# A decode training step with two attention and two MLP layers: five query-weight chunks instead of four stay on chip between the two backward passes

## The chip, the cores and the metric

The kernel runs on one core of a Trainium2 chip. The metric is the device time of one execution in microseconds (us). A core has five engines with queues of their own: PE (matrix multiply, with its weight loads shown as PEld), DVE (vector), ACT (scalar), POOL and SP. SP does no arithmetic here; it issues most of the transfers between the large memory and the on-chip memory. Sixteen DMA engines carry every transfer, whichever engine issued it. The profile counts times from the start of the span.

## What is computed

One token passes through attention A, MLP B, attention A and MLP B again, with shared weights, and then the gradients of everything are taken. Cut to what matters:

```python
def A(x, k_cache, v_cache, wq, wo):          # D=1024, 32 heads of 128, 4 groups, window 4096
    q = x @ wq                               # wq: 1024 x 4096
    k, v = the last 4096 rows of each cache
    o = softmax(q k^T * 128**-0.5) v
    return o @ wo                            # wo: 4096 x 1024

def B(x, w1, b1, w2):                        # w1: 1024 x 3584, w2: 3584 x 1024
    h = x @ w1 + b1
    return (h * tanh(softplus(h))) @ w2

x = x + A(layernorm(x)); x = x + B(layernorm(x))
x = x + A(layernorm(x)); x = x + B(layernorm(x))
# outputs: x, and by the chain rule from grad_out the gradients of
# x, k_cache, v_cache, wq, wo, w1, b1, w2 (all bf16)
```

The cache gradients have the full length of 32768 rows. Outside the window of 4096 they are zero, and those zeros have to be written: 56 stores of 1 MB.

## The kernel before

**The weights come in chunks of 1 MB.** wq is cut into eight chunks of 128 rows (all 4096 columns), wo into eight of 512 rows, w2 into seven of 512 rows. A chunk of wq, wo or w2 lands in a slot of `ring_t`, eight slots of 8 KB in each of the 128 partitions. The class `Ring` (line 38) keeps a list of loads in a fixed order, each with a key such as `("q", 2, 3)`: chunk 3 of the third use of wq. `pump` (line 51) issues the next load on SP's queue when a slot is free in the program's order; the slot's last reader is waited for by SP itself. `release` (line 80) gives a slot back and pumps. `keep` (line 76) gives a chunk a new key and no slot back, so a chunk stays on chip. `lend` (line 86) adds slots: when w1 is no longer needed, three slots are cut from its memory. In the profile a load into `ring_t` is called `ring<-in_...`, a load into a lent slot `W<-in_...`.

**The order of the loads** is written out once (lines 270 to 290). Its end is what matters here: wq for the second attention's backward pass (`("q", 2, t)`, eight chunks), w2 for the first MLP's backward pass (`("2", 1, c)`, seven), wo for the first attention's backward pass (`("o", 3, c)`, eight), and the rest of wq for the first attention's backward pass (`("q", 3, t)`). The chunks of wq that `KEEP_Q2` (line 268) lists are not loaded this last time.

**The stages of the second half, in the order of the program.**

1. The second attention's backward pass, `attn_bwd(1, ...)` (line 960). Its last part is the wq loop of line 918, which multiplies each chunk with the query gradient. For this the chunk's 128 x 128 blocks have to be transposed: PE transposes eight blocks into PSUM (line 452), DVE or ACT copies them back over the chunk in its slot (`evac`, lines 305 and 308, whichever has less work by a running tally), and PE multiplies with them (line 471). That is called turning a chunk. A chunk has four groups of eight blocks. In chunks 0 and 1 all four are turned; in chunks 2 to 7 one group is left and goes as a row dot on DVE (line 429), and three are turned. `later` (line 436) holds a few products back, so that PE has transposes to do while a copy runs. After its products a chunk is released, or, if `KEEP_Q2` lists it, kept in its turned form; its key goes into `turned_q`.
2. The first MLP's backward pass, first loop (line 1105): for each of the seven chunks of w2, the forward product that is still owed (`mlp_out`, line 700: 32 weight loads and matmuls), then `flush`, which runs the products and releases that were held back, then the same chunk's gradient by two row dots and two turned groups. So a chunk's slot comes back only after the next chunk's `mlp_out`.
3. The first MLP's backward pass, second loop (`dn_b0`, line 840) with w1, which is on chip. During it SP issues small copies that gather rows for the outer products (lines 986, 786, 828).
4. `ring.lend(lent)` (line 1119): three more slots.
5. The first attention's backward pass, `attn_bwd(0, ...)`: the wo loop (line 865), two stages with the cached keys and values, and the wq loop again (line 918). A chunk whose key is in `turned_q` is only multiplied.
6. The outer products that make the weights' and caches' gradients (from line 1180), copied out of PSUM by DVE and ACT and stored by SP.

**The zeros** are issued on POOL's queue by `zeros(n, after)` (line 256), so many at each of several points of the program, each after a named value is ready: 3 while the second attention's wq loop begins, 1 at the end of it, 2 before `dn_b0`, and 19 later.

Of the kernel before, what the change touches and what calls it, by code (L numbers as in the profile page):

```python
# [93 lines left out]
def kernel(  # L94
# [135 lines left out]
    def want_q(k, ts=range(8)):  # L230
        for t in ts:
            ring.want(("q", k, t), wq_v[:, t, :], [P, J])

    def want_o(k, cs=range(8), homes=()):
        for c in cs:
            own = homes[c].rearrange("p (k d) -> p k d", k=4) if c < len(homes) else None
            ring.want(("o", k, c), wo_v[:, c], [P, 4, D], own, [("K", c)] if own is not None else [])
# [27 lines left out]


    KEEP_Q = (5, 6, 7)
    KEEP_Q2 = (4, 5, 6, 7)
    EARLY_2 = (0, 1)
    MID_2 = (2, 3)  # L270
    W1S = W1[:].rearrange("p t f -> p (t f)")
# [17 lines left out]
    want_o(3)  # L289
    want_q(3, [t for t in range(8) if t not in KEEP_Q2])  # L290
    ring.pump()
# [344 lines left out]
    def conv(n, eng=None):  # L636
        for _ in range(n):
            conv_ev(conv_pe(1), eng)
# [318 lines left out]
    def dq3():  # L957
        zeros(3, DQC[:, 0, 1:2])

    g2 = attn_bwd(1, sA1, g3, ("o", 1), ("q", 2), KEEP_Q2,  # L960
                  dict(do=lambda c: conv(1), dp=dp3, dq=dq3, dn=lambda t: None),
# [256 lines left out]
```

## Time and profile before

| | |
|---|---|
| three runs | 458.6, 459.16, 459.25 us (median 459.16) |
| the profiled execution | 458.38 us, of which the span is 456.6 us |
| PE, DVE, ACT, POOL busy | 322.4, 257.5, 204.6, 38.5 us |
| bytes moved | 183.56 MB: 83.94 read, 98.62 written |
| second attention's wq loop | from 223 to 243 us |
| first MLP's w2 loop | from 246 to 275 us |
| `dn_b0` | from 276 to 283 us |
| first attention's wo loop | from 286 to 305 us |
| first attention's wq loop | from 318 to 334 us |
| last arithmetic instruction ends | 422.5 us |

How to read the profile: the page divides the span into 40 slices of 11.4 us. A digit is the busy share of an engine in a slice in tenths, and 9 stands for 90% or more. DMA is the mean busy share of the sixteen DMA engines. The granted clock is the share of its full rate that PE was given. The chain of waits starts at the last instruction and goes back, at each step to what released the instruction, or to the one before it on its engine. A timeline line gives the start, the duration, the engine, the line of the program, the operation, what it writes and reads, and how often it stands there in a row; in brackets is the idle time of the engine before it and what ended it. A line of SPq is the issue of a transfer on SP's queue, not the transfer. A transfer's landing is told by sixteen completion marks, one from each DMA engine; its reader waits for the last of them.

### The profile page before, as it was taken

Reading aid. Unit: us, or ns where it says so; the run is one execution under the profiler, and the core shown is the slowest. Engines: PE = TensorE matmul, PEld = TensorE weight load, DVE = VectorE, ACT = ScalarE, POOL = GpSimd, SP = SyncE. Lnnn points to the kernel's source line nnn. Section 1 sums busy time; section 2 is a strip of 40 time slices with the busy share of each in tenths; the row PEclk is TensorE's granted clock in tenths of the full one; section 3 lists DMA queues with packets and bytes.
Section 4 is the critical chain, followed back from the end, with each engine's and each line's share of the span. In section 5 each row is a group of like instructions: output and inputs, shape, how many; then the busy total and the mean of one; then the engine's idle time right before and its main releaser. Section 6 shows DMA issues by size and latency. Waiting matters only on the chain.

```text
span 456.6 us, 13914 instructions
## 1 busy us (share of the span) xinstructions
PE 322.4 (71%) x6225; PEld 258.9 (57%) x6225; DVE 257.5 (56%) x506; ACT 204.6 (45%) x239; POOL 38.5 (8%) x84
## 2 busy tenths in 40 slices
PE   3836543456698898987798868988978988899000
PEld 3735433456597897987798768976922222345000
DVE  4504737278441265846286556763769999989000
ACT  2501001011054277752283542761669999998000
POOL 1000000002031222102100001022130000000000
PEclk9955555555555599978598555995955555555555
DMA  8999999989999999999999979999999999999995
GB/s 334 421 421 421 417 421 419 420 317 422 421 417 423 419 415 416 393 416 418 421 423 425 417 284 342 390 391 420 421 417 420 416 421 419 424 421 418 407 408 227
DMA packets 28377, 183.56 MB, mean 402 GB/s; under 512 B 3706, under 2 KB 3734, under 8 KB 9494
## 3 DMA queue, kind: packets, MB, share of 16 engines
q1 hardware_dynamic: 20162, 123.94, 66.6%
q0 software_dynamic: 8064, 58.72, 31.1%
q8 instruction: 48, 0.79, 0.6%
q14 instruction: 11, 0.09, 0.0%
q10 hardware_dynamic: 92, 0.02, 0.0%
HBM read 83.94 MB, written 98.62 MB: 400 GB/s over the span
## 4 chain that ended last, share of the span: by engine, by line
PE 37%; DMA 28%; DVE 11%; ACT 10%; issue 6%; SPq 0%; ACTq 0%; DVEq 0%
DMA ring<-in_B_w_dram 13%; PE BIG L452 9%; PE TP L471 5%; DMA ring<-in_A_wq_dram 5%; DMA W<-in_A_wo_dram 4%; DMA W<-in_B_w_dram 4%; ACT ring L308 4%; PE wide L1073 4%; PE wide L1022 3%; DVE junk L429 3%; DMA W<-in_A_k_cache_dram 2%; ACT W L308 2%; PE BIG L628 2%; PE MV L648 2%; ACT KT L308 2%
## 5 line engine op out<-in xcount | busy, mean ns | idle before, releaser
L308 ACT COPY ring<-BIG 128x1024 bf16<-128x1024 bf16 x51 | 50.4, 1015 | 45.5 <-PE BIG L452 20.1
L452 PE MATMUL BIG<-ident_bf,ring 128*128 128x128 bf16 x664 | 58.8, 247 | 0.5 <-ACT ring L308 0.3
L1022 PE MATMUL wide<-W 2*128 2x512 bf16 x228 | 52.1, 598 | 9.3 <-ACT W L308 1.9
L452 PEld LDWEIGHTS <-ring 128*128 128x128 bf16 x768 | 55.9, 113 | 1.1 <-issue 0.6
L429 DVE CUSTOM_DVE_ANT_0 junk<-ring,SC 128x1024 bf16<-128x1024 bf16 x32 | 38.9, 1215 | 9.8 <-DMA ring<-in_B_w_dram 9.4
L1022 PEld LDWEIGHTS <-W 2*128 2x128 bf16 x240 | 12.5, 102 | 44.0 <-issue 42.9
L305 DVE CAST ring<-wide 128x1024 bf16<-128x1024 f32 (+1 forms) x29 | 33.7, 1201 | 3.2 <-PE wide L1022 1.4
L471 PEld LDWEIGHTS <-ring 128*128 128x128 bf16 x864 | 30.0, 98 | 7.2 <-issue 3.4
L308 ACT CAST ring<-wide 128x1024 bf16<-128x1024 f32 (+1 forms) x35 | 32.9, 1018 | 1.3 <-PE wide L1073 0.5
L264 POOL DMA_DIRECT2D out_dram<-zt x56 | 29.7, 534 | 37.6 <-DMA out_dram<-zt 37.1
L305 DVE COPY ring<-BIG 128x1024 bf16<-128x1024 bf16 x32 | 21.8, 690 | 17.7 <-PE BIG L452 15.7
L429 DVE CUSTOM_DVE_ANT_0 junk<-ring,DSX 128x1024 bf16<-128x1024 bf16 x24 | 29.4, 1224 | 0.8
L648 PE MATMUL MV<-NB,W 128*128 128x1 bf16 x448 | 16.4, 172 | 14.8 <-DMA W<-in_B_w_dram 12.8
L308 ACT COPY KT<-BIG 128x1024 bf16<-128x1024 bf16 x14 | 13.8, 1008 | 26.7 <-PE BIG L628 25.2
L648 PEld LDWEIGHTS <-W 128*128 128x128 bf16 x448 | 15.8, 118 | 15.6 <-DMA W<-in_B_w_dram 13.4
L514 PE MATMUL MV<-NA,ring 128*128 128x1 bf16 x512 | 15.1, 165 | 12.6 <-DMA ring<-in_A_wq_dram 11.2
L308 ACT COPY W<-BIG 128x1024 bf16<-128x1024 bf16 x21 | 20.7, 1014 | 5.0 <-PE BIG L452 4.4
L452 PE MATMUL BIG<-ident_bf,W 128*128 128x128 bf16 x288 | 22.3, 221 | 0.3 <-issue 0.3
L514 PEld LDWEIGHTS <-ring 128*128 128x128 bf16 x512 | 14.6, 104 | 13.3 <-DMA ring<-in_A_wq_dram 11.9
L305 DVE CAST VS<-wide 128x1024 bf16<-128x1024 f32 (+1 forms) x17 | 19.7, 1188 | 3.6 <-PE wide L1022 3.0
L1073 PE MATMUL wide<-W 32*128 32x256 bf16 x128 | 20.9, 402 | 0.9 <-ACT ring L308 0.8
L308 ACT CAST KT<-wide 128x1024 bf16<-128x1024 f32 x20 | 20.4, 1032 | 1.8 <-PE wide L1022 0.9
(258 smaller groups left out, 538.5 us busy)
## 6 DMA issues: line engine op xcount, KB each, us to landing
out_dram<-zt POOLq DMA_DIRECT2D x56, 1024.0 KB, 20.3
ring<-in_A_wq_dram SPq DMA_DIRECT2D x24, 1024.0 KB
ring<-in_A_wo_dram SPq DMA_DIRECT2D x14, 1024.0 KB
ring<-in_B_w_dram SPq DMA_DIRECT2D x13, 1024.0 KB
W<-in_A_wo_dram SPq DMA_DIRECT2D x10, 1024.0 KB
W<-in_B_w_dram SPq DMA_DIRECT2D x8, 896.0 KB
out_dram<-ring SPq DMA_DIRECT2D x7, 1024.0 KB
out_dram<-ring SPq DMA_DIRECT2D x13, 512.0 KB
```

The costliest lines, as they stand in the source:

```text
L264: nc.gpsimd.dma_start(dst, zt[:])
L305: nc.vector.tensor_copy(dst, src)
L308: nc.scalar.copy(dst, src)
L429: nc.vector.tensor_tensor_reduce(out=out, in0=a, in1=vec, scale=1.0, scalar=acc if i else 0.0, op0=ALU.mult, op1=ALU.add, accum_out=acc)
L452: nc.tensor.transpose(b[:, i * P:(i + 1) * P], block(w, i) if block else w[:, i * P:(i + 1) * P], ident_bf[:])
L471: nc.tensor.matmul(out, lhsT=w[:, i * P:(i + 1) * P], rhs=rhs_of(i), start=fresh[0], stop=last and i == n - 1, skip_group_check=True)
L514: nc.tensor.matmul(q_ps[:, h:h + 1], lhsT=ch[:, h * P:(h + 1) * P], rhs=NA[:, t, l:l + 1], start=(k == 0 and h == 0), stop=(k == TD - 1), ...
L628: nc.tensor.transpose(b[:, i * P:(i + 1) * P], T[:, g, 8 * b8 + i, :], ident_bf[:])
L648: nc.tensor.matmul(h_ps[:, fb:fb + 1], lhsT=f_block(W1[:, t], fb), rhs=NB[:, t, l:l + 1], start=(t == 0 and fb == 0), stop=(t == TD - 1), ...
L1022: nc.tensor.matmul(b[:, 512 * i:512 * i + 512], lhsT=R[at:at + 2, lo:lo + P], rhs=R[at:at + 2, ro + 512 * i:ro + 512 * i + 512], start=Tru ...
L1073: nc.tensor.matmul(b[:, k * 256:(k + 1) * 256], lhsT=RT[32 * g:32 * g + 32, a, tp, :], rhs=YS[32 * g:32 * g + 32, :], start=True, stop=Tru ...
```

## The change

`KEEP_Q2` gets one more member, chunk 3:

```diff
     KEEP_Q = (5, 6, 7)
-    KEEP_Q2 = (4, 5, 6, 7)
+    KEEP_Q2 = (3, 4, 5, 6, 7)
     EARLY_2 = (0, 1)
```

The tuple is used in two places. In the list of loads, the last use of wq asks for chunks 0 to 2 and no longer for chunk 3:

```python
    want_q(3, [t for t in range(8) if t not in KEEP_Q2])
```

In the second attention's wq loop, chunk 3 is kept in its turned form, so its slot isn't given back there; the first attention's wq loop multiplies with it without turning it, and gives the slot back:

```python
            if t in wq_keep:
                ring.keep(key, ("q", 3, t))
                turned_q.add(("q", 3, t))
            else:
                later(lambda key=key: ring.release(key))
```

From the second attention's wq loop to the first's, five of the eight slots are taken, and three are left to the chunks of w2 and wo, until three more are lent. By the order of the instructions on each engine, PE has 24 transposes and 24 weight loads less, DVE one copy and ACT two copies less, all in the first attention's wq loop. SP issues the seven loads of w2 as before, then three loads of wo instead of four before the small copies of stage 3, and after the lend five loads of wo and three of wq instead of four and four. The instructions of POOL are the same in number and order.

## The prediction

> **What bounds the kernel now.** I read the page's slices first, then the stretches around its only hole, then the chain of waits, then the timeline of the load queue. The page shows transfers nearly everywhere:
>
> ```profile
> span 456.6 us, 13914 instructions
> ...
> DMA  8999999989999999999999979999999999999995
> GB/s 334 421 421 421 417 421 419 420 317 422 421 417 423 419 415 416 393 416 418 421 423 425 417 284 342 390 391 420 421 417 420 416 421 419 424 421 418 407 408 227
> ```
>
> Only slices 24 to 27 (262 to 308 us) fall clearly short in the second half. Stretches (columns: us; busy us of PE, PEld, DVE, ACT, POOL; granted clock; DMA share; GB/s):
>
> ```profile
> 256.00:260.00 4.00, 2.94 (x59) 2.67 (x56) 2.23 (x4) 2.61 (x3) 0.00 (x0) 0.50 1.01 422
> 260.00:264.00 4.00, 3.17 (x64) 2.91 (x64) 2.46 (x4) 1.05 (x3) 0.00 (x0) 0.50 0.98 395
> 264.00:268.00 4.00, 2.71 (x62) 2.71 (x63) 2.46 (x4) 1.28 (x3) 0.00 (x0) 0.50 0.91 340
> 268.00:272.00 4.00, 2.14 (x57) 1.87 (x55) 1.55 (x3) 1.62 (x2) 0.00 (x0) 0.50 0.65 254
> 272.00:276.00 4.00, 2.38 (x33) 1.96 (x31) 1.52 (x6) 1.93 (x2) 0.31 (x2) 0.50 0.78 279
> 276.00:280.00 4.00, 4.00 (x127) 3.85 (x126) 3.35 (x9) 0.25 (x1) 0.93 (x2) 0.50 0.86 231
> ...
> 316.00:336.00 20.00, 17.64 (x360) 15.47 (x361) 13.01 (x28) 9.36 (x13) 4.93 (x12) 0.76 1.01 420
> 336.00:424.00 88.00, 74.51 (x394) 26.55 (x393) 77.38 (x72) 81.00 (x92) 2.80 (x6) 0.50 1.01 419
> 424.00:448.00 24.00, 0.00 (x0) 0.00 (x0) 0.00 (x0) 0.00 (x0) 0.00 (x0) 0.50 1.02 407
> ```
>
> The reader sees two regimes. From 288 us to 448 the sixteen DMA engines are full, and from 424 on no engine computes: stores alone set the end. From 260 to 288 they are not full, and something else sets the time. The chain of waits names it (start, us, what):
>
> ```profile
> 235.15 20.49 DMA ring<-in_B_w_dram
> ...
> 257.28 12.99 DMA ring<-in_B_w_dram
> 270.33 1.01 PE MV L700 x32
> ```
>
> These are chunks of w2 for the first MLP's backward loop (line 1105). Call them c0 to c6. c3 is issued at 235.15 and starts its matmuls at 255.69; c6 is issued at 257.28 and starts at 270.33. The load queue around them:
>
> ```profile
> 235.15 0.33 SPq L71 DMA_DIRECT2D ring<-in_B_w_dram  x1
> 250.66 0.33 SPq L71 DMA_DIRECT2D ring<-in_B_w_dram  x1
> 253.97 0.33 SPq L71 DMA_DIRECT2D ring<-in_B_w_dram  x1
> 257.28 0.33 SPq L71 DMA_DIRECT2D ring<-in_B_w_dram  x1
> ```
>
> c0 to c3 take the slots of wq chunks 0 to 3 (229.57 to 235.15); c4, c5, c6 take those of c0, c1, c2. A slot comes back about 1.55 us after the next chunk's matmuls begin (255.69 to 257.28, 270.33 to 271.84 for the slot that a wo chunk takes), because line 1108 flushes only there. The zero stores from POOL compete: the one issued at 245.83 lands 25.1 us later.
>
> **The change, part by part.**
>
> *Removed: one wq load.* 1.05 MB, at 421 GB/s 2.5 us of all engines. It pays only where the engines are full for want of nothing else. The instruction order shows where it goes: before line 1119 lends three slots, SP issues three wo loads instead of four, and after it five wo and three wq loads, where it issued four and four. So the saturated stretch keeps its eight loads, and the missing megabyte comes out of the stretch that has holes already. I count 0; its bound is -2.5.
>
> *Removed: three turns of wq chunk 3 in the first attention's wq loop (line 918).* PE loses 24 transposes and their weight loads, DVE one copy, ACT two. By the rows of that loop:
>
> ```profile
> 324.17 0.61 PE L452 MATMUL BIG<-ident_bf,ring 128*128 128x128 bf16 x8
> 324.24 0.69 DVE L305 COPY ring<-BIG 128x1024 bf16<-128x1024 bf16 x1 [0.32 <-PE BIG L452]
> 324.81 1.93 ACT L308 COPY ring<-BIG 128x1024 bf16<-128x1024 bf16 x2 [0.28 <-PE BIG L452]
> ```
>
> PE loses 3 x 0.61 = 1.83, DVE 0.69, ACT 1.93 us. A turned chunk takes 2.14 us there (row dots at 324.84 and 326.99), a kept one 1.27 (the row dots from 329.13, 330.38, 331.65 on, DVE's own pace), so the loop ends 0.87 us sooner. What covers it is the store and zero traffic of 316 to 336 (share 1.01): worth 0; without that cover -0.9.
>
> *Moved: five of eight ring slots are taken from 235 us on, so three and not four rotate.* c3 must wait for c0's slot: issued at 250.66, 15.5 us later than before. c0, c1, c2 and the releases at 250.66 and 253.97 don't depend on it. How long does c3 then take? The trace shows a load into an empty queue under the same zero traffic: wq chunk 0, issued at 188.91, whose completion marks (one for each DMA engine) run from 197.8 to 200.4, thus 8.9 to 11.5 us. Lower bound: the wo chunk issued at 262.20, when most engines had no zeros left, first mark at 266.6, thus 4.4. The consumer waits for the last mark, and one engine is some 8 us behind the others with zeros (the last zero's marks: fifteen by 262.7, one at 270.9), so I take 11.5: c3 starts at 262.2, not 255.69.
>
> The Trainium skill ("DMA: Bandwidth & Descriptors", Queues, rings and completion order) says that each engine takes turns between the queues that have work, and its Specifications give about 0.6 us to the first byte for SP's path. By that, an estimate: c3 would land after 0.6 us and one shared 5 us turn, near 256.3, and almost nothing would be lost (rival A). The wq row, twice as slow, speaks against it; the even sharing itself the trace bears out (loads land every 5 us at 255.7, 260.7, 265.3, 270.3 beside zeros).
>
> What is late next: PE's own pace. One chunk costs it 1.01 (L700) + 0.56 (L471) + 1.87 (L452) = 3.45 us at the halved clock. c4, issued at 253.97, is right behind c3. c5 is issued 1.55 us after c3 starts, at 263.8, c6 at 267.2; the zeros, which are fixed in number, ran alone while loads were away and are then nearly gone, so 4.4 us each suffice (268.2, 271.6). Hence starts at 262.2, 265.65, 269.1 and 272.55: c6 is 2.2 us late. Bounds: 0.6 (c3 after 6.9 us: 1.9 to the first packet, as below, and one shared turn of 5; then the slowest engine merely does the same packets in another order, and c6 comes after the last zero at 270.9) and 4 (c5 and c6 each another 1 us late in landing).
>
> Behind SP's waits for these slots stand, in order, the wo loads, the row copies of lines 986, 786 and 828, and the lent slots' loads. All move by the same 2.2 us, and none has a taker earlier: the first wo chunk, issued after c5's start (270.7) and not at 262.2, is first turned at 282.77 + 2.2. After the lend every chunk is one place later in the queue. wo chunk 6 then takes the place of chunk 7 (marks to 299.2, first use 299.55), chunk 7 that of wq chunk 0 (marks to 301.7, first use 302.24). That fits by 0.3 to 0.5 us; I count 0.
>
> *What of the 2.2 reaches the end.* The first lent load is issued at 284.69 and its packets can begin 1.9 us later (4.4 less 2.5 of transfer), at 286.6; after the change at 288.8. But the slowest engine was before still busy with zeros until 287.7 (their last mark), so it loses only 288.8 - 287.7 = 1.1 us, and it ends the kernel (last marks 453.9 on the second slowest, 455.3 on the slowest). From there on bytes are equal. The others lose 2.2 and end at 456.1; the slowest at 456.4.
>
> Sum: 0 + 0 + 1.1. The profiled execution took 458.38 us with a span of 456.6, so 459.5; the median of the runs is 459.16, 0.78 above it: **460.3 us**.
>
> **The rivals.**
>
> *A: the late load is absorbed.* If c3 takes its turn within 6.9 us (257.5), c6 is 0.6 us late, and the slowest engine gains 1.1 less 0.6: 459.16 - 0.5 = 458.7, no change to tell. For it: strict alternation on the slowest engine, which is never idle from 235 to 288. Against: the wq row.
>
> *B: the bytes count (not slower).* If the end is set by all bytes together, the missing 1.05 MB is worth 2.5 us: 456.7. For it: share 0.9 or more in nearly all slices. Against: the hole of 260 to 288, whose stretches are already 6.7 us short of 421 GB/s in sum; a load less there widens the hole unless the loop itself gets quicker.
>
> *C: the wo loads arrive late as well.* The margins of 0.3 and 0.5 us after the lend fail, PE stalls in the loop of line 865, slots come back later and the engines run dry near 300 us, where they are at 324 GB/s already: 2 us more, 462.5. Against: loads of 5 chunks are outstanding by then.
>
> That the change does nothing is excluded: the order has one wq load and 24 transposes fewer.
>
> **How the numbers follow.** Forecast 0.42, A 0.34, B 0.16, C 0.08. A measurement of this kernel can tell about 0.2% (0.9 us) from no change. Of the forecast, 0.03 lies within that bound, of A 0.02 below it. Faster: 0.16 + 0.02 = 0.18. Within: 0.32 + 0.03 = 0.35. Slower: 0.39 + 0.08 = 0.47. The range takes A and the bounds of the delay (0.6 to 4 us, thus -0.5 to +2.9, and 0.8 more below for part of B): 457.9 to 462.1; the forecast's own is 459.4 to 461.3.
>
> **What would show it.** Right: c3 issued near 250.7 and its matmuls at 260 to 263; chunk starts after it 3.4 us apart, no longer waiting for loads but PE-paced; the lent loads 1 to 3 us later; DMA share in 268 to 284 lower than before; from 290 on the same 420 GB/s; the first attention's wq loop 0.9 us shorter without effect. Wrong: c3 landing before 257.5 (A), an end earlier by 2 us with the lent loads on time (B), or PE waiting for wo loads between 290 and 305 (C).

## The result, and the profile after

| | before | after |
|---|---|---|
| median of ten runs each, on one chip | 458.98 us (458.41 to 459.9) | 460.16 us (459.74 to 462.1) |
| ratio | 1 | 1.0034, 95% interval 1.0022 to 1.0046 |
| profiled execution: span | 456.6 us | 458.3 us |
| w2 chunk c3: issued, first matmul | 235.15, 255.69 | 250.86, 259.91 |
| last w2 chunk c6: first matmul | 270.33 | 271.73 |
| first lent load issued | 284.69 | 287.27 |
| end of the first attention's wo loop | 305.6 | 308.8 |
| first attention's wq loop (line 332 to line 402) | 317.58 to 334.24 | 321.78 to 337.05 |
| last completion mark of all | 455.3 | 457.0 |

The kernel became slower: by 0.34% in the ratio (1.6 us), by 1.2 us in the medians and by 1.7 us in the spans of the two profiles. Two cautions for reading what follows. The ratios of the record aren't the ratios of the medians. And only one execution of each kernel is profiled: those of e1, e5 and e8 are the fastest of their runs, 1.2 to 1.4 us below the median, and the w2 loop starts anywhere from 244.2 us (e1) to 252.7 us (e2), though the instructions ahead of it are the same in these two and in the kernel after (247.0). A difference of a few us between single rows of two profiles is therefore not by itself the edit's doing. The slices of the page after:

```profile
span 458.3 us, 13855 instructions
...
DMA  8999999989999999999999779999999999999996
GB/s 331 421 420 419 420 420 418 420 317 421 420 417 421 422 413 415 410 400 420 423 424 423 294 275 339 347 404 422 420 417 416 416 419 420 422 420 415 407 408 252
```

There is still one hole in the second half, but it begins a slice earlier. Slice 23 (252 to 263 us) moved 417 GB/s before and moves 294 now. The stretches of the profile after (us; busy us of PE, PEld, DVE, ACT, POOL; granted clock; DMA share; GB/s):

```profile
256.00:260.00 4.00, 0.10 (x4) 0.09 (x4) 0.00 (x1) 1.17 (x2) 0.00 (x0) 0.50 0.88 358
260.00:264.00 4.00, 3.08 (x64) 2.82 (x64) 2.46 (x4) 1.73 (x2) 0.00 (x0) 0.50 0.51 150
264.00:268.00 4.00, 3.03 (x64) 2.91 (x64) 2.46 (x4) 0.83 (x2) 0.00 (x0) 0.50 0.53 203
268.00:272.00 4.00, 3.37 (x75) 3.24 (x74) 2.85 (x5) 2.13 (x3) 0.00 (x0) 0.50 0.80 274
272.00:276.00 4.00, 3.46 (x69) 3.03 (x66) 2.06 (x4) 2.61 (x4) 0.00 (x0) 0.50 0.86 313
276.00:280.00 4.00, 2.77 (x84) 2.69 (x84) 2.29 (x9) 0.41 (x1) 1.25 (x3) 0.50 0.93 295
...
288.00:292.00 4.00, 4.00 (x53) 3.60 (x51) 2.17 (x4) 1.49 (x3) 0.00 (x0) 0.66 0.90 292
316.00:336.00 20.00, 16.91 (x437) 15.86 (x437) 12.34 (x22) 5.98 (x8) 3.70 (x10) 0.67 1.01 419
336.00:424.00 88.00, 76.89 (x404) 27.33 (x403) 77.77 (x79) 82.62 (x96) 4.02 (x9) 0.50 1.01 418
424.00:448.00 24.00, 0.23 (x2) 0.00 (x0) 1.49 (x2) 0.58 (x1) 0.00 (x0) 0.50 1.02 408
```

From 256 to 260 PE does almost nothing (0.10 us of 4; before 2.94): it waits for c3. From 260 to 268 PE works about as much as before, but the DMA engines stand half idle (0.51 and 0.53, before 0.98 and 0.91): with three slots there is nothing more that SP may issue, and the zeros are used up but for the last completion mark of the last piece (267.2). From 316 us on the two profiles are alike: full engines, then stores alone. The timeline of the w2 loop, with the first lines of line 700 for each chunk. Before, c3 to c6:

```profile
255.69 1.01 PE L700 MATMUL MV<-AC,ring 128*128 128x1 bf16 x32
260.69 1.02 PE L700 MATMUL MV<-AC,ring 128*128 128x1 bf16 x32 [1.75 <-DMA ring<-in_B_w_dram]
265.29 1.01 PE L700 MATMUL MV<-AC,ring 128*128 128x1 bf16 x32 [1.44 <-DMA ring<-in_B_w_dram]
270.33 1.01 PE L700 MATMUL MV<-AC,ring 128*128 128x1 bf16 x32 [1.86 <-DMA ring<-in_B_w_dram]
```

After, the issues of SP and c2 to c6:

```profile
250.86 15.96 SPq L71 DMA_DIRECT2D ring<-in_B_w_dram  x4
252.84 1.01 PE L700 MATMUL MV<-AC,ring 128*128 128x1 bf16 x32 [0.33 <-DMA ring<-in_B_w_dram]
259.91 1.01 PE L700 MATMUL MV<-AC,ring 128*128 128x1 bf16 x32 [3.90 <-DMA ring<-in_B_w_dram]
264.97 1.02 PE L700 MATMUL MV<-AC,ring 128*128 128x1 bf16 x32 [1.88 <-DMA ring<-in_B_w_dram]
268.77 1.01 PE L700 MATMUL MV<-AC,ring 128*128 128x1 bf16 x32 [0.63 <-DMA ring<-in_B_w_dram]
...
271.73 1.04 PE L700 MATMUL MV<-AC,ring 128*128 128x1 bf16 x32
```

c3 is issued at 250.86, when c0's slot comes back. Its sixteen completion marks run from 256.1 to 259.9, so it took 5.2 us on the quickest DMA engine and 9.0 on the slowest, and PE waited 3.9 us. The marks spread over the whole time between (the last two came at 259.5 and 259.9). Behind the loop SP issues the small copies and then the lent loads:

```profile
280.63 1.68 SPq L986 DMA_DIRECT2D W<-W  x2
282.42 0.84 SPq L786 DMA_DIRECT2D W<-dr_AC  x1
283.32 0.89 SPq L786 DMA_DIRECT2D W<-dr_NB  x1
284.26 0.71 SPq L786 DMA_DIRECT2D W<-dr_OC  x1
285.01 0.50 SPq L786 DMA_DIRECT2D W<-dr_NA  x1
285.61 1.54 SPq L828 DMA_DIRECT2D W<-W  x2
287.27 2.29 SPq L71 DMA_DIRECT2D W<-in_A_wo_dram  x3
```

The copies begin 1.74 us later than before (278.89 there) and the first lent load 2.58 later: SP spends 6.64 us on the copies and not 5.80.

**Two ways to add it up.** The first is the prediction's: the end of the span follows the issue of the first lent load, 171.9 us behind it before (456.6 - 284.69) and 171.0 after. The second is an own count over the packet records: the time in which all sixteen engines would have carried what they carried, and the rest, idle time. In the hole, from 236 to 308 us, the mean idle time grew from 3.7 to 7.7 us; one load of 2.5 us fell away; 4.0 - 2.5 = 1.5 us, against 1.7 in the span. (A plain sum of the packet times, which reaches a share of 1.02 where the engines are full, gives 2.9 and 6.9: the same growth.) In the other rows of the table below this second sum misses the span by up to 1.4 us, in e2 by 2.1 and in e3 by 4.4, so it tells where time is lost and proves no price. The argument rests on the first.

### The profile page after: what moved, and what is told of

The parts are those of the page before. It is cut to its first block, busy times and chain, and to the rows that moved or that the text cites. A ratio compares the mean times of both kernels' runs of the same rounds, so it can differ in the third digit from the quotient of the medians.

```text
span 458.3 us, 13855 instructions
## 1 busy us (share of the span) xinstructions
PE 316.8 (69%) x6201; PEld 253.1 (55%) x6201; DVE 256.9 (56%) x505; ACT 202.8 (44%) x237; POOL 38.5 (8%) x84
## 5 line engine op out<-in xcount | busy, mean ns | idle before, releaser
L308 ACT COPY ring<-BIG 128x1024 bf16<-128x1024 bf16 x49 | 48.4, 1014 | 46.7 <-PE BIG L452 22.5
L452 PE MATMUL BIG<-ident_bf,ring 128*128 128x128 bf16 x624 | 52.8, 240 | 1.5 <-issue 1.2
L452 PEld LDWEIGHTS <-ring 128*128 128x128 bf16 x712 | 49.6, 110 | 2.2 <-issue 1.7
L471 PEld LDWEIGHTS <-ring 128*128 128x128 bf16 x832 | 28.4, 98 | 8.9 <-issue 4.8
L305 DVE COPY ring<-BIG 128x1024 bf16<-128x1024 bf16 x29 | 19.8, 689 | 16.6 <-PE BIG L452 15.1
L648 PE MATMUL MV<-NB,W 128*128 128x1 bf16 x448 | 16.5, 172 | 15.1 <-DMA W<-in_B_w_dram 7.6
L514 PEld LDWEIGHTS <-ring 128*128 128x128 bf16 x512 | 14.8, 104 | 14.2 <-DMA ring<-in_A_wq_dram 11.2
```

The lines of the kernel that those rows point to most:

```text
L305: nc.vector.tensor_copy(dst, src)
L308: nc.scalar.copy(dst, src)
L452: nc.tensor.transpose(b[:, i * P:(i + 1) * P], block(w, i) if block else w[:, i * P:(i + 1) * P], ident_bf[:])
L471: nc.tensor.matmul(out, lhsT=w[:, i * P:(i + 1) * P], rhs=rhs_of(i), start=fresh[0], stop=last and i == n - 1, skip_group_check=True)
L514: nc.tensor.matmul(q_ps[:, h:h + 1], lhsT=ch[:, h * P:(h + 1) * P], rhs=NA[:, t, l:l + 1], start=(k == 0 and h == 0), stop=(k == TD - 1), ...
L648: nc.tensor.matmul(h_ps[:, fb:fb + 1], lhsT=f_block(W1[:, t], fb), rhs=NB[:, t, l:l + 1], start=(t == 0 and fb == 0), stop=(t == TD - 1), ...
```

## The experiments

Ratios are to the kernel before, with 95% intervals. "Idle" is the own count from 236 to 308 us in the profiled execution.

| run | ratio | first lent load | span | span less lent load | idle |
|---|---|---|---|---|---|
| before | 1 | 284.69 | 456.6 | 171.9 | 3.7 |
| after | 1.0034 (1.0022 to 1.0046) | 287.27 | 458.3 | 171.0 | 7.7 |
| e1_slot_withheld | 1.0087 (1.0068 to 1.0107) | 286.45 | 459.8 | 173.4 | 7.3 |
| e2_turn_again | 1.0039 (1.0023 to 1.0055) | 288.75 | 459.9 | 171.2 | 7.4 |
| k6_six_kept | 1.0337 (1.0305 to 1.0368) | 300.33 | 471.7 | 171.4 | 22.4 |
| k3_three_kept | 1.0059 (1.0046 to 1.0072) | 288.88 | 459.9 | 171.0 | 4.8 |
| e5_zeros_after_chunk_4 | 1.0023 (1.0004 to 1.0042) | 284.61 | 456.4 | 171.8 | 6.6 |
| e6, the same on before | 1.0021 (0.9999 to 1.0043) | 287.32 | 457.9 | 170.6 | 6.2 |
| e10_two_zeros_later | 1.0055 (1.0041 to 1.0069) | 288.51 | 459.4 | 170.9 | 8.0 |
| e11, the same on before | 1.0016 (0.9999 to 1.0034) | 286.68 | 457.7 | 171.0 | 5.8 |
| e7_zeros_into_hole | 1.0047 (1.0034 to 1.0059) | 290.71 | 459.0 | 168.3 | 7.3 |
| e8, the same on before | 1.0015 (0.9996 to 1.0035) | 290.02 | 456.0 | 166.0 | 3.7 |
| e3_copies_behind_lent_loads | 1.0172 (1.0156 to 1.0189) | 284.68 | 464.3 | 179.6 | 9.5 |
| e9_copies_on_act_queue | 1.0049 (1.0033 to 1.0065) | 287.91 | 458.9 | 171.0 | 8.7 |

### The slot alone

The kernel before, in which chunk 3's slot isn't given back by the second attention's wq loop, though the chunk is loaded and turned again later:

```diff
@@ line 935
             if t in wq_keep:
                 ring.keep(key, ("q", 3, t))
                 turned_q.add(("q", 3, t))
+            elif l == 1 and t == 3:
+                ring.keep(key, "held")
             else:
```

> The kernel before, but the slot of wq chunk 3 is not given back after the second attention's wq loop; chunk 3 is loaded again and turned again as before, so nothing is saved. My theory (the starved w2 loop makes the lent loads late, and the end follows the start of the saturated stretch; the saved load comes out of the hole): the w2 loop as in the changed kernel (first row dot after it within 0.7 us of 277.1, first lent load near 287.3), but nine loads after the lend and not eight, so 2.5 us over the changed kernel, 462.7. Rival (the bytes are what count, the slot costs nothing): as before, 459.0. Rival (the later arithmetic sets the end): 460.2 plus the 1.4 us by which the changed kernel's wq loop is shorter, 461.6.

Measured: 1.0087, 462.82 us. The theory's time came (462.7), with the first lent load 0.8 us sooner than it had it. The w2 loop looks like that of the changed kernel (c3, then the lent loads):

```profile
258.26 1.01 PE L700 MATMUL MV<-AC,ring 128*128 128x1 bf16 x32 [4.03 <-DMA ring<-in_B_w_dram]
...
286.45 2.27 SPq L71 DMA_DIRECT2D W<-in_A_wo_dram  x3
```

PE waits 4.03 us for c3, and the lent loads come 1.8 us later than before. Here nine megabyte loads instead of eight stand behind the lend, and the span ends 173.4 us behind the first of them, 2.4 more than after. In this profile, the fastest of e1's runs, the end is 3.2 us later than before: 1.8 from the lend, the rest from the ninth load. By the ratio the slot by itself costs 0.87%, 4.0 us, and what the change takes away (a load and three turns) gives back 1.0087 - 1.0034, 2.4 us with about 1 us either way.

### The turns alone

The changed kernel, where chunk 3 is nevertheless turned a second time in the first attention's wq loop:

```diff
-                if key in turned_q:
+                if key in turned_q and not (l == 0 and t == 3):
```

> The changed kernel, but the first attention's wq loop turns chunk 3 once more (24 transposes, 3 copies; the chunk is then in its first form, so the gradient of x is computed from the wrong blocks). Theory (arithmetic there is covered by stores): as the changed kernel, 460.2 within 0.5. Rival (the arithmetic after the lend sets the end): the loop 1.4 us longer and the end with it, 461.6.

Measured: 1.0039 (the x gradient is then made from wrongly turned blocks) against 1.0034 without it; the intervals cover each other, and the rival's 1.4 us more (1.0065) lies above both. The median is 461.35 us, which alone would be nearer to the rival: the seven runs fall into two groups, three at 459.3 to 460.2 us and four at 461.4 to 461.7. The profile, of the slowest run, speaks for the theory. Its wq loop took 17.3 us (321.52 to 338.80) instead of 15.27, and yet the end stands 171.2 us behind the first lent load, against 171.0 without the turns. What this run lost, it lost ahead of the edit: its w2 loop began at 252.74 us, 5.7 later than in the profile after. So the 2.4 us that came back are put down to the load.

### One slot less still, and one more

`KEEP_Q2 = (2, 3, 4, 5, 6, 7)`, where two slots turn over, and `KEEP_Q2 = (5, 6, 7)`, where the w2 loop has five.

> Six chunks of wq kept (2 to 7), so two slots rotate through the w2 loop; one more load and three more turns are saved. Theory (a slot's round trip of release, issue and landing sets the loop): each chunk waits for the one two before it, 1.55 us after the next one's start plus 4.4 to 9 us, so some 6 to 7 us a chunk from chunk 2 on; the loop ends 12 to 15 us later than with five kept and the end moves with it, 470 to 475. Rival (bytes): 2.5 us less, 457.7.

Measured: 1.0337, 473.99 us, as the theory had it. With two slots PE waits for each load from c2 on. Three of the five:

```profile
257.26 1.01 PE L700 MATMUL MV<-AC,ring 128*128 128x1 bf16 x32 [7.17 <-DMA ring<-in_B_w_dram]
264.74 1.02 PE L700 MATMUL MV<-AC,ring 128*128 128x1 bf16 x32 [4.32 <-DMA ring<-in_B_w_dram]
271.08 1.01 PE L700 MATMUL MV<-AC,ring 128*128 128x1 bf16 x32 [3.17 <-DMA ring<-in_B_w_dram]
```

The lent loads come 15.6 us later than before, the end 15.1.

> The other direction: three wq chunks (5, 6, 7) stay turned, the w2 loop turns over one slot more than in the kernel before, and one chunk more is loaded and turned in the first attention's wq loop. Theory (the slot cost 4.0 us in the step from four to five chunks because it starved the w2 loop; from four to three there is little starvation to remove, since chunk 3 of the kernel before waits for zeros as much as for its slot, while the load more costs its 2.4 us behind the lent loads): 459.0 to 461. Rival (a slot is worth about the same at every step): one slot more gives back 4.0 and takes 2.4, 456.5 to 458. Rival (bytes and turns are all that counts): 461.4 and more.

Measured: 1.0059, 461.63 us: above the theory's range, and where the rival "bytes and turns" had it, but not by that rival's way alone. The loop was hardly starved, as the theory had it: waits for loads sum to 0.8 us, and the idle time of 260 to 284 us fell from 3.5 to 1.6. (In this profile the loop also began 4.9 us later than before, at 251.71, which by itself leaves the loads more time.) The theory was wrong about the queue behind it. A new hole opened when the copies were due (the 12 us stretches of that kernel, then SP's waits in 280 to 300 us: total, times, longest):

```profile
272.00:284.00 12.00, 10.27 (x264) 9.40 (x262) 7.61 (x24) 3.72 (x5) 1.24 (x3) 0.50 0.94 336
284.00:296.00 12.00, 11.61 (x220) 11.28 (x216) 8.49 (x23) 7.08 (x8) 0.00 (x0) 0.84 0.74 288
```

```profile
SPq L828 <- DMA ring<-in_A_wo_dram: 3.0, 1, 3.0
```

Five wo loads now stand ahead of the copies, and the second copy of line 828 waits 3.0 us until the last of them has landed, though it reads nothing of it. By the time, the load more was paid in full and the slot gave nothing at the end; how much of that is this wait and how much the late start of the loop, one profile doesn't tell. Of three, four, five and six kept chunks, four is the best.

### Taking the zeros out of the w2 loop's way

In the changed kernel and in the one before, the zeros that are issued around 221 and 246 us are issued behind chunk 4 of the w2 loop:

```diff
-        zeros(3, DQC[:, 0, 1:2])
...
-    zeros(1, g2)
...
     for c in range(7):
...
+        if c == 4:
+            zeros(4, da0[:, 4 * c:4 * c + 1])
```

> The changed kernel, but the four zero stores issued between 220 and 247 us (three at the query gradient, one at the w2 loop's start) are issued after chunk 4 of the w2 loop. Theory (the zeros that stand in the engines are what makes the late load of c3 slow): c3 lands 4.4 to 5 us after its issue and not 5.2 to 9, its matmuls start near 255.5, the loop runs at PE's pace of 3.4 us a chunk and ends some 6 us sooner, the zeros then fill the hole, and the end comes 3 to 6 us sooner: 454 to 457. Rival (three slots are too few by themselves, whatever else moves): c3 as late as 259 to 260, and the end within 1 us of 460.2.

Measured: 1.0023, 459.48 us. The first half of the theory came, the second did not. c3, issued at 249.24, had all its marks by 253.9 and started at 254.00: 4.8 us instead of 9.0. The loop ended 6 us sooner. But the lent loads were no sooner than before the change (284.61, there 284.69). The moved zeros now filled the engines when the small copies were due (share 1.02 in 276 to 280 us, before 0.86), and the issue of one copy took 4.29 us:

```profile
276.79 0.33 SPq L786 DMA_DIRECT2D W<-dr_OC  x1
277.16 4.29 SPq L786 DMA_DIRECT2D W<-dr_NA  x1
281.55 2.94 SPq L828 DMA_DIRECT2D W<-W  x2
284.61 3.50 SPq L71 DMA_DIRECT2D W<-in_A_wo_dram  x3
```

> The kernel before with the same four pieces of zeros moved behind chunk 4 of the w2 loop, so that no zeros stand in the way of that loop's loads in either kernel of the pair. Theory (a slot less costs time through loads that are issued late and then land slowly beside zeros; the load left out is worth its 2.4 us whenever the engines are full): without zeros the loop of the changed kernel is hardly starved (chunk 3 landed in 4.8 us there), so of the slot's 4.0 us little is left, and this kernel, which has one load more, is level with the changed kernel under the same edit or slower by up to 2.4 us: 459.5 to 461.9. Rival (the slot costs its 4.0 us by itself, by the later issue, zeros or not): this kernel is 1.5 us ahead of it, 457.9, and would be ahead of the kernel before as well.

Measured: 1.0021, 459.65 us, level with the changed kernel under the same edit, where the theory had it. By the theory the slot then costs about what the load saves, 2.4 us, and the other 1.6 us of its 4.0 come from zeros that a late load meets. That isn't shown. The margin of 1.5 us to the rival is no larger than the intervals, and the two profiles don't help: the loops end alike (the first copy is issued at 274.35 in the changed kernel, at 274.54 here), but that of the changed kernel had begun 2.2 us sooner; and behind the loop they differ in something that neither reasoning has, for here one copy held SP for 6.74 us, there for 4.29, and the lent loads come 2.7 us later here.

```profile
277.99 6.74 SPq L786 DMA_DIRECT2D W<-dr_NA  x1
```

A smaller dose, two pieces of zeros behind chunk 3 instead. The edit takes one of the three that are issued around 221 us and the one of 246 us; that they were issued at 188.91 us, as the expectation says, is a slip (a load of wq is issued then):

> The changed kernel, with two pieces of the first projection gradient's zeros moved: of those that were issued at 188.91 us, two wait until chunk 3 of the w2 loop is done, so that chunk 3's load meets fewer zeros. Theory (the end follows the first lent load; the load of chunk 3 lands late because the slowest engine is still storing zeros): chunk 3 starts at 255 to 257 us and not at 259.9, the w2 loop ends 3 to 5 us sooner, the lent loads are issued at 282 to 284 us and not at 287.3, and the end stands 171 to 172 us behind them: 455 to 457.5. Rival (as in the run with all zeros moved, the zeros fill the engines while SP's small copies are to be issued, and the lent loads get no further forward than 284.6): 459 to 460.

> The kernel before with the same two pieces of zeros moved. Theory: here the w2 loop has its five slots and starts chunk 3 at 255.7 us, behind fewer zeros it starts it 2 to 3 us sooner; the lent loads are issued at 282 to 284.7 us: 456.5 to 459. Rival (zeros beside SP's small copies cost as much as they give): 459 to 460. If the theory of the slot holds, this kernel stays 0 to 2 us ahead of the same edit on the changed one.

Measured: 461.41 us (1.0055) and 459.34 us (1.0016). The changed kernel missed both ranges, upwards. Fifteen of c3's marks came by 254.9, the last only at 258.1; the zeros that were left had fifteen marks by 251.0 and the last at 257.4. And the two pieces, issued at 259.7, met c6's load, which took from 262.89 to 273.3:

```profile
258.11 1.02 PE L700 MATMUL MV<-AC,ring 128*128 128x1 bf16 x32 [2.27 <-DMA ring<-in_B_w_dram]
...
273.33 1.01 PE L700 MATMUL MV<-AC,ring 128*128 128x1 bf16 x32 [4.21 <-DMA ring<-in_B_w_dram]
```

The kernel before with this edit came out in the rival's range (459 to 460), not in the theory's: no gain, with the lent loads at 286.68. It is 2 us ahead of the changed one, as expected if the slot costs.

### Filling the hole

Two of the four pieces of zeros that are issued around 310 us go behind chunk 5 of the w2 loop, in both kernels:

```diff
+        if c == 5:
+            zeros(2, da0[:, 4 * c:4 * c + 1])
...
-        zeros(4)
+        zeros(2)
```

> The changed kernel, but two of the four zero stores at line 1150's stage (about 310 us) are issued after chunk 5 of the w2 loop (about 271 us), into the hole. Theory (the saturated stretch sets the end and the hole before it is lost time): 2.1 MB, 5 us of all engines, leave the saturated stretch; the hole of 270 to 290 us holds some 3 us of idle engine time, so the end comes 2 to 3 us sooner, 457 to 458, unless the zeros make the wo loads and with them SP's queue late, which gives part of it back. Rival (the lent loads' time alone sets the end, whatever fills the hole): 460 or later.

> The kernel before with the same two zero stores moved into its hole. Its hole is 3.6 us of all engines, not 7.6, and its slowest engine has none. Theory: at most 1 to 3 us sooner, 456 to 458, and the changed kernel with the same edit is then within 1 us of it or better, since the hole no longer eats the load that was saved. Rival (the slot costs by itself, not through the hole): the changed kernel with the edit stays 1.2 us behind this one or more.

Measured: 460.79 us (1.0047) and 459.07 us (1.0015): no gain in either, against both theories. The changed kernel stays 1.7 us behind, which is what the second rival said (1.2 or more): filling the hole doesn't take away what the slot costs. Less work is left behind the lent loads (the end follows after 168.3 and 166.0 us), but these come 3.4 and 5.3 us later, since the copies wait again. In the changed kernel:

```profile
283.62 5.16 SPq L786 DMA_DIRECT2D W<-dr_NA  x1
288.88 1.72 SPq L828 DMA_DIRECT2D W<-W  x2
290.71 1.69 SPq L71 DMA_DIRECT2D W<-in_A_wo_dram  x3
```

### The small copies out of the way

Two runs on the changed kernel: the four copies of line 786 issued behind the lent loads (the four calls of `take_back` stand behind `ring.lend(lent)`), and the copies issued by ACT's queue:

```diff
-        nc.sync.dma_start(ROWS[base:base + 2, off:off + ...], r)
+        nc.scalar.dma_start(ROWS[base:base + 2, off:off + ...], r)
```

> The changed kernel, but the four copies of line 786 are issued by SP after the three lent loads and not before them. Theory (the end follows the lent loads): they are issued 2 to 3 us sooner (near 285), the engines' idle time of 286 to 290 us (1.1 us of all sixteen) goes, and the end comes 1.1 us sooner, 459.1; at most 2 us sooner. Rival (the end follows the arithmetic of the w2 loop and of what comes after it): the loop is as late as before, so 460.2.

Measured: 1.0172, 466.6 us: far outside both numbers. The lent loads did come 2.6 us sooner (284.68), and then the queue stood still behind them (SP's waits, 280 to 308 us: total, times, longest; line 982 is line 986 of the other kernels):

```profile
SPq L71 <- DMA out_dram<-W: 6.1, 1, 6.1
SPq L982 <- DMA W<-in_A_wo_dram: 4.6, 2, 2.9
SPq L786 <- DMA W<-in_A_wo_dram: 3.4, 1, 3.4
```

A small copy waits for a megabyte load that it has nothing to do with, and a load waits 6.1 us for a store. The share of 296 to 308 us falls to 0.76. The end is no longer 171 us behind the first lent load but 179.6: the rule holds only while the loads behind it follow without a gap.

> The changed kernel, but the four copies of line 786 are issued on ACT's queue at the same place of the program, not on SP's. Theory (SP's queue ahead of the lent loads is part of what makes them late): the lent loads are issued 1.5 to 3 us sooner than at 287.3, and the end comes about 1.1 us sooner, 459.1. Rival (their issue waits for arithmetic or landings in any case): no change, 460.2.

Measured: 1.0049, 460.66 us: the rival. SP issued the copies of line 828 at 284.60, 1 us sooner than after (it had waited 2.3 us for ACT's copy of line 826), but the lent loads only at 287.91. What held them the waits of SP say (280 to 293 us):

```profile
SPq L71 <- DMA W<-dr_AC: 1.7, 1, 1.7
```

The first lent load is counted on the semaphore on which the copy that ACT issued at 280.23 is counted, and that copy's last marks came at 287.8.

No version was found that is faster than the kernel before.

## Why the prediction was right, step by step

**What bounds the kernel.** Right. In ten of the thirteen changed kernels the end came 170.6 to 173.4 us behind the first lent load; the two of them that differ most in their lend (284.61 and 300.33) end 171.8 and 171.4 behind it. In e7 and e8 it came sooner, with two pieces of zeros less behind the lend. Only e3, which breaks the chain of loads there, leaves the rule. The nine of the ten with eight loads behind the lend end 170.6 to 171.8 us behind it; e1, with nine loads, is the 173.4.

**The removed load: 0 and the slot: +1.1.** Right as a sum, and only as a sum. The forecast rise was 1.1 us; measured were 1.2 in the medians, 1.6 by the ratio and 1.7 in the profiles. The prediction counted eight loads behind the lend in both kernels, which is so. But the slot alone pushes a ninth load behind the lend (e1), and the removal takes it away again: +4.0 and -2.4 in the measured order. Whoever would have priced the load by the bytes alone (rival B, 456.7) had a real term of the right size and overlooked the larger one. Rival B falls as an outcome: the ratio's lower bound is 1.0022.

**The three turns: 0.** Right, as far as e2 can tell. The wq loop is 1.4 us shorter (0.87 was forecast), the stores of 316 to 336 us cover it at a share of 1.01, and with the turns put back the end stands as far behind the first lent load as without them.

**c3's load: 11.5 us, start 262.2.** The mechanism is right, the size isn't: issued 0.2 us later than forecast, it took 9.0 us and started at 259.91. The 11.5 were taken because one engine was thought to be some 8 us behind the others; c3's last mark came only 0.4 us behind the fifteenth, so its lateness was shared by many engines. The marks show what lay between the two views weighed there. By the Trainium skill ("DMA: Bandwidth & Descriptors", Queues, rings and completion order), where the engines take turns between queues, c3 was estimated near 256.3, and its first mark came at 256.1. For the quickest engine the trace agrees; the reader waits for the slowest, and that took 3.8 us more. Rival A, which needed c3 by 257.5, fell on this.

**PE's pace behind it: 3.45 us a chunk, c6 2.2 us late.** Mostly wrong. c4 did not follow c3 at PE's pace: it started 5.06 us later, having waited 1.88 us for its own load (issued 254.36, last mark 264.9, the fifteenth 262.8). c5 waited 0.63 us for its load too (issued 261.43, last mark 268.7), 3.8 us behind c4, and only c6 came at PE's pace, 2.96 us later. So the loads stayed late for longer than forecast, while c3 had come sooner: c6 was 1.4 us late and not 2.2. The hole lies elsewhere as well. The DMA share of 268 to 284 us was to fall and rose, from 0.82 to 0.88; it is in 256 to 268 us that it fell, from 0.97 to 0.64.

**What stands behind on SP's queue: all by the same 2.2 us.** This is the term that was left out. The copies' delay was not constant: they began 1.74 us late, and their issue took 0.84 us longer. That this fills what c6 fell short, so that the lent load was 2.58 us late and close to the 2.2, is luck: c3 was put 2.3 us too late, the three chunks behind it 1.5 us too close together, and the copies at no further delay.

**What reaches the end: +1.1.** Mis-sized: +1.7 in the profile. The slowest engine's zeros, which ended at 287.7 before, now end at 289.2, just when lent packets can begin (287.27 + 1.9 = 289.2); 1.5 us of it is that shift. That the slowest engine loses less than the others, which is the prediction's reasoning here, the marks of the fourth load behind the lend show: its first mark came 2.4 us later than before (299.2, before 296.8), its last 1.7 us later (300.9, before 299.2).

**wo chunks 6 and 7 fit by 0.3 to 0.5 us: 0.** Right. Chunk 6 had landed at 300.9 us and was first touched at 302.5; chunk 7 had landed at 303.4 and was first touched at 305.1. The uses had moved back further than the landings. PE does stand still for 0.9 us at 300.2, but in the middle of a group of products with chunk 5, which had landed at 298.4, and the profile names nothing that it waited for (PE's waits, 284 to 312 us: total, times, longest):

```profile
PE TP L471 <- issue: 1.3, 2, 0.9
```

So rival C's wait isn't there. With this pause the loop ends 3.3 us late, but the engines are full from 292 on (in 296 to 308 us the share is 1.02, before 1.01), so it costs nothing.

## What to carry to other kernels

In a kernel whose end is set by transfers, ask of a saved load what it frees and of a taken buffer what it starves: here, in the step from four to five kept chunks, a slot of 1 MB was worth 4.0 us where a load of 1 MB was worth 2.4, because it decides how early the next load can be issued; in the step from four to three it gave nothing. A load issued late beside queued stores should be priced by its last completion mark, not its first. And before filling a hole in the transfers, look at what has to be issued in it: the hole was where small copies got through, and every megabyte put there came back as a later load.

## What the runs showed of the hardware that was not expected

- The issue of a small copy can take long on the queue itself: line 786's cost 0.34 to 1.00 us each before, and single ones 3.80 (e8), 4.29 (e5), 5.16 (e7) and 6.74 us (e6) with more zeros queued. All of it stands in front of the loads that follow on SP. Full engines alone don't do it (before, the share of 280 to 284 us was 1.00 as well); what holds the issue isn't shown.
- SP's queue waits for the landing of transfers that the next one doesn't depend on (3.0 us in k3, 3.4, 4.6 and 6.1 in e3, 1.7 in e9). In the traces SP's and ACT's transfers are counted on eight semaphores in turn, and each of these waits is for the transfer that used the same semaphore before: in e3 a load issued at 304.59 and ACT's store issued at 300.22, in e9 the first lent load and ACT's copy. That the reuse of semaphores is the cause is read from this order; it wasn't tried with more of them.
- One of a zero store's sixteen marks can lag far behind, though every engine has a share of the piece: for the piece issued at 246.6 us in the changed kernel the first fifteen marks run from 252.4 to 261.3, the last comes at 267.2. That it is always the same engine is likely and not shown, since the marks don't name theirs. Some loads beside the zeros share the lag (c3 in e10: fifteen marks by 254.9, the last at 258.1; c4 after: 262.8 and 264.9), others don't (c3 after: 259.5 and 259.9). With no zeros beside it, c3 in e5 had all sixteen within 0.4 us (253.5 to 253.9).
